# Sparse attention into a rational-activation MLP on one core: value matmuls grouped by row tile, casts let go batch by batch, first batch first, smaller groups and four banks at the ends

## The chip, the cores and the metric

The kernel runs on one core of one Trainium2 chip. The metric is the device time of one execution in microseconds (us). Profiles show the span of one execution, which is about 2 us shorter than the device time of the same run (595.4 against 597.3 us for the kernel before). All times in the text are medians unless they are read from one trace.

Engines: PE is TensorE, DVE is VectorE, ACT is ScalarE, POOL is GpSimd, SyncE (SP) issues DMA. "Granted clock" is the share of full speed that the profile shows for TensorE. A transfer "lands" when its semaphore reports it complete; it "starves" when it takes far longer to land than the same transfer does elsewhere in the trace, because others run beside it.

## The reference

Eight batches of 8 heads, 576 tokens, 64 columns. Heads 0 to 3 see a local band of 32 tokens, heads 4 to 7 every 32nd token. The result, 4608 x 512, goes through a two-layer MLP with a rational function in between.

```python
scores = (q @ k.T) / sqrt(D)                       # per batch and head
mask_local   = (rel >= 0) & (rel < 32)             # heads 0..3
mask_strided = (rel >= 0) & (pos_k % 32 == pos_q % 32)   # heads 4..7
attn = softmax(where(mask, scores, -1e9)) @ v      # B=8, H=8, S=576, D=64
x = attn.transpose(0, 2, 1, 3).reshape(4608, 512)
h = x @ w_in                                       # 512 -> 2048
P = a0 + a1*h + a2*h**2 + a3*h**3
Q = 1 + |b0|*|h| + |b1|*h**2
out = (P / (Q + 1e-6)) @ w_out                     # 2048 -> 512, fp32
```

## The kernel before

A list scheduler in the kernel file takes operations with an engine, dependences, an assumed cost and a priority key, and from them fixes the order of instructions on each engine. A change of a cost or of a dependence can therefore move many instructions.

For each of eight batches: POOL issues three casts (q, k, v from fp32 to bf16 copies in DRAM). SyncE loads from these copies: `ql` and `kl` re-layouts in DRAM (8 x 72 KB) and four transposes `qL`/`kL` from them for the local heads, four transposes `qS`/`kS` for the strided heads, 17 value loads. Then come scores on PE with Exp on ACT, five row tiles T = 0 to 4 of value matmuls into `psA`, a division on DVE into `XR`, and a DMA transpose of each tile into `XT`. Chunk c of the dense part is batch c's first 512 tokens; chunk 8 collects the 64 left-over tokens of all batches. "mm1" is `XT` times `Win` into `psH`; ACT evicts to `HB`; a chain of nine DVE operations (d1 to d9) with Ln and Exp on ACT makes the gate; "mm2" multiplies by `Wout` into `psO`.

```python
# the scheduler's model of a DMA: fixed latency after issue
end = free[e] + op.cost
op.end = end + op.lat

# all casts may start at once; so may the weights (POOL queue)
for b in range(B):
    for nm, s_, d_ in (("q", q, qc), ("k", k, kc), ("v", v, vc)):
        ...
        key = (b - 3) * P if b else -1000 + len(cast)
        add("POOL", <cast of the whole tensor of batch b>, [], 1.2, key, g, 5.0)
# Win: 4 loads, key -900; Wout: 4 loads, key 0.3 * P; neither waits for anything

def attend(b, evs):                     # matmul order inside one row tile T
    ...
    for h in range(4):                  # local heads
        makers.append(<128-row (T<4) or 64-row (T=4) matmul into psA[:, h]>)
        if T > 0:
            makers.append(<32-row matmul into the same psA[:, h]>)
    for h in range(4):                  # strided heads
        for g in range(4):
            if T < 4:
                makers.append(<128-row matmul into psA[32*g:32*g+32, 4+h]>)
            else:
                makers.append(<128-row matmul, 16 columns>)
                makers.append(<16-row matmul into the same place>)

# dense1: two groups of G = 8 column tiles per chunk; d9 writes a separate gate tile GB
# dense2: for each of four row blocks m: 16 matmuls into the one bank psO,
#         eviction on ACT, then 4 (last chunk: 8) stores issued by POOL
```

The softmax here doesn't subtract the row's maximum and nothing guards it: scores larger than these inputs give would overflow.

## Time and profile before

| | before |
|---|---|
| device time, median (lowest to highest) | 597.88 us (597.57 to 598.76), 3 runs |
| first score matmul | 113.5 us |
| first mm1 matmul / first DVE chain starts | 178.6 / 213.9 us |
| last chain ends / last store has landed / span ends | 567.3 / 591.3 / 595.4 us |
| DVE busy, PE busy over the span | 303.3, 390.4 us |

The page's second part cuts the span into 40 slices of 14.9 us; each digit is the busy share in tenths. Kernel before:

```profile
PE   0000000233349259899999999999999999998572
DVE  1000000000011049988869668768868986999910
PEclk9999999999999559999979979979979979999987
DMA  8999997546665542334625535532211211111202
```

For about seven slices DMA is nearly full and PE has nothing to do; DVE's first chain comes in slice 15. From slice 16 to near the end PE is full.

SyncE's timeline of the kernel before (start, duration in us, operation) shows what the full DMA did to the first loads:

```profile
7.51 40.92 SPq L461 DMA_DIRECT2D ql<-qc  x4
48.48 11.91 SPq L472 DMA_TRANSPOSE qS<-qc  x2
...
133.79 2.65 SPq L461 DMA_DIRECT2D ql<-qc  x4
```

The same four 72 KB loads occupy SyncE for 40.9 us while all casts are in flight, and 2.65 us later.

Windows of the kernel before (stretch, its length, then busy us of each engine with the number of instructions, granted clock, DMA share, GB/s):

```profile
core 0: us, PE busy (x) PEld busy (x) DVE busy (x) ACT busy (x) POOL busy (x), PEclk, DMA share, GB/s
0.00:114.00 114.00, 0.48 (x2) 0.13 (x2) 2.18 (x17) 1.28 (x1) 17.29 (x36) 1.00 0.96 187
380.00:425.00 45.00, 43.98 (x338) 21.75 (x343) 34.33 (x30) 31.15 (x35) 10.14 (x18) 0.92 0.30 55
515.00:567.00 52.00, 39.48 (x174) 16.40 (x175) 51.79 (x32) 39.33 (x39) 20.94 (x32) 0.97 0.17 41
```

In the middle stretch one batch takes 45 us and PE is busy for 44 of them, so PE sets the pace there; DMA is at 0.30. In the last one DVE is.

The same 45 us, counting only instructions that touch `psA` (the value matmuls of one batch):

```profile
core 0: us, PE busy (x) PEld busy (x) DVE busy (x), PEclk, DMA share, GB/s
380.00:425.00 45.00, 10.13 (x132) 6.63 (x132) 4.81 (x11) 0.92 0.30 55
```

PE's timeline of the kernel before around such a block: one block of 16 matmuls of the same shape, then the fifth row tile, where 128-row and 16-row matmuls alternate, and the matmuls behind it:

```profile
426.55 0.30 PE L520 MATMUL psA<-vs,ES 128*32 128x65 bf16 x16
...
433.17 0.20 PE L520 MATMUL psA<-vs,ES 128*16 128x65 bf16 x1
433.30 0.19 PE L520 MATMUL psA<-w,ES 16*16 16x65 bf16 x1
...
437.06 0.22 PE L520 MATMUL psA<-vs,ES 128*16 128x65 bf16 x1
437.21 0.22 PE L520 MATMUL psA<-w,ES 16*16 16x65 bf16 x1
437.77 1.49 PE L520 MATMUL psH<-XT,Win 128*128 128x512 bf16 x3 [0.34 <-issue]
439.05 1.91 PE L520 MATMUL psO<-Wout,GB 128*128 128x512 bf16 x4
```

Sixteen matmuls of one shape take 0.30 us; alternating ones start 0.13 to 0.15 us apart, so the 40 of the fifth tile take 5.3 us. It is not the second write into the same place of `psA` that costs: the step from a 16-row matmul to the next 128-row one, which writes another place, takes as long (0.12 to 0.15 us). Behind them a group of four 512-column matmuls takes 1.91 us where the usual is 1.03: the granted clock is 0.50 from 434.7 to 441.5 us, although PE was busy for 8.54 of the 8.70 us before that, at 1.00.

The tail of the kernel before, POOL's timeline:

```profile
574.71 15.25 POOL L799 DMA_DIRECT2D out_dram<-OS  x32 [11.80 <-issue]
```

The last 32 stores are issued one after the other, 7.4 us after the last chain's end (567.3).

### The profile page before, as it was taken

Reading aid. Unit: us, or ns where it says so; the run is one execution under the profiler, and the core shown is the slowest. Engines: PE = TensorE matmul, PEld = TensorE weight load, DVE = VectorE, ACT = ScalarE, POOL = GpSimd, SP = SyncE. Lnnn points to the kernel's source line nnn. Section 1 sums busy time; section 2 is a strip of 40 time slices with the busy share of each in tenths; the row PEclk is TensorE's granted clock in tenths of the full one; section 3 lists DMA queues with packets and bytes.
Section 4 is the critical chain, followed back from the end, with each engine's and each line's share of the span. In section 5 each row is a group of like instructions: output and inputs, shape, how many; then the busy total and the mean of one; then the engine's idle time right before and its main releaser. Section 6 shows DMA issues by size and latency. Waiting matters only on the chain.

```text
span 595.4 us, 6854 instructions
## 1 busy us (share of the span) xinstructions
PE 390.4 (66%) x2801; PEld 185.2 (31%) x2848; DVE 303.3 (51%) x259; ACT 272.3 (46%) x301; POOL 114.6 (19%) x196
## 2 busy tenths in 40 slices
PE   0000000233349259899999999999999999998572
PEld 0000000011124134454544544444454444443220
DVE  1000000000011049988869668768868986999910
ACT  0000000120104009976756757757756757988510
POOL 9200000000000000022213112212213222434336
PEclk9999999999999559999979979979979979999987
DMA  8999997546665542334625535532211211111202
GB/s 175 212 217 215 210 221 120 98 77 103 110 106 83 102 79 39 84 51 91 122 49 96 97 62 89 92 61 46 59 31 36 45 35 36 36 36 35 54 22 49
DMA packets 151839, 53.34 MB, mean 90 GB/s; under 512 B 145408, under 2 KB 147968, under 8 KB 151040
## 3 DMA queue, kind: packets, MB, share of 16 engines
q1 hardware_dynamic: 142848, 25.10, 25.3%
q0 software_dynamic: 8960, 27.80, 21.9%
q8 instruction: 22, 0.36, 0.3%
q14 instruction: 9, 0.07, 0.0%
HBM read 47.10 MB, written 28.31 MB: 127 GB/s over the span
## 4 chain that ended last, share of the span: by engine, by line
PE 46%; SPq 30%; DVE 10%; issue 4%; ACT 4%; POOL 3%; DMA 2%; DVEq 0%; POOLq 0%
PE psH L520 16%; PE psO L520 15%; PE psA L520 10%; SPq L461 9%; SPq L465 8%; SPq L472 5%; PE psS L520 4%; SPq L478 3%; POOL out_dram L799 3%; DVE GB L756 2%; DVE T L751 2%; DVE T L747 2%; ACT UU L737 1%; SPq L495 1%; DMA qc<-in_q_dram 1%
## 5 line engine op out<-in xcount | busy, mean ns | idle before, releaser
L791 POOL DMA_DIRECT2D out_dram<-OS x128 | 82.1, 647 | 462.5 <-ACT OS L784 462.1
L520 PE MATMUL psO<-Wout,GB 128*128 128x512 bf16 x551 | 147.3, 396 | 18.1 <-ACT OS L784 9.3
L520 PE MATMUL psH<-XT,Win 128*128 128x512 bf16 x558 | 146.9, 399 | 12.6 <-DMA XT<-XR 6.5
L716 ACT ACTIVATE HB<-psH 128x512 bf16<-128x512 f32 x144 | 82.5, 600 | 63.7 <-PE psH L520 62.6
L520 PE MATMUL psS<-MS,IDN 128*128 128x432 bf16 (+1 forms) x48 | 14.3, 386 | 130.7 <-DMA kL<-kl 128.8
L650 DVE RECIPROCAL RC<-psA 128x8 f32<-128x8 f32 x40 | 8.2, 205 | 180.0 <-PE psA L520 180.0
L567 ACT ACTIVATE ES<-psS 128x864 bf16<-128x864 f32 (+1 forms) x24 | 20.4, 849 | 143.9 <-PE psS L520 143.7
L520 PEld LDWEIGHTS psO<-Wout,GB 128*128 128x128 bf16 x576 | 54.8, 101 | 88.0 <-ACT OS L784 16.0
L520 PEld LDWEIGHTS psH<-XT,Win 128*128 128x128 bf16 x576 | 56.0, 102 | 81.0 <-issue 11.8
L737 ACT ACTIVATE UU<-UU,cst 128x2048 bf16<-128x2048 bf16 x36 | 71.7, 2001 | 4.2 <-DVE UU L730 4.2
L740 ACT ACTIVATE UU<-UU 128x2048 bf16<-128x2048 bf16 x36 | 68.8, 1911 | 0.1
L520 PEld LDWEIGHTS psS<-MS,IDN 128*128 128x128 bf16 x48 | 3.7, 101 | 134.4 <-DMA kL<-kl 128.9
L756 DVE TENSOR_TENSOR GB<-T,UU 128x4096 bf16<-128x4096 bf16 x18 | 41.1, 2284 | 4.1 <-ACT UU L740 3.9
L652 DVE TENSOR_TENSOR XR<-psA,RC 128x512 bf16<-128x512 f32 x40 | 27.4, 686 | 30.5 <-DMA XT<-XR 30.2
L751 DVE TENSOR_TENSOR T<-T,HB 128x4096 bf16<-128x4096 bf16 x18 | 41.1, 2283 | 0.3
L747 DVE TENSOR_TENSOR T<-T,HB 128x4096 bf16<-128x4096 bf16 x18 | 40.9, 2273 | 0.1
L730 DVE TENSOR_TENSOR UU<-UU,ZZ 128x4096 bf16<-128x4096 bf16 x18 | 40.9, 2271 | 0.0
L784 ACT ACTIVATE OS<-psO 128x512 f32<-128x512 f32 x36 | 21.4, 595 | 42.3 <-PE psO L520 42.2
L520 PE MATMUL psA<-vs,ES 128*32 128x65 bf16 (+1 forms) x640 | 37.1, 203 | 0.0
L724 DVE TENSOR_SCALAR ZZ<-HB 128x4096 uint16<-128x4096 uint16 x18 | 22.0, 1221 | 16.9 <-ACT HB L716 16.9
L520 PE MATMUL psA<-w,ES 16*16 16x65 bf16 x128 | 26.4, 206 | 0.0
L744 DVE TENSOR_SCALAR T<-HB,coef 128x4096 bf16<-128x4096 bf16 x18 | 24.1, 1339 | 0.0
(53 smaller groups left out, 295.2 us busy)
## 6 DMA issues: line engine op xcount, KB each, us to landing
out_dram<-OS POOLq DMA_DIRECT2D x128, 64.0 KB, 2.0
qc<-in_q_dram POOLq DMA_DIRECT2D x8, 576.0 KB, 43.6
kc<-in_k_dram POOLq DMA_DIRECT2D x8, 576.0 KB, 45.9
vc<-in_v_dram POOLq DMA_DIRECT2D x8, 576.0 KB, 48.2
ql<-qc SPq DMA_DIRECT2D x32, 72.0 KB, 2.8
kl<-kc SPq DMA_DIRECT2D x32, 72.0 KB, 2.8
Win<-in_moe_w_in_dram POOLq DMA_DIRECT2D x4, 512.0 KB, 17.0
Wout<-in_moe_w_out_dram POOLq DMA_DIRECT2D x4, 512.0 KB, 46.0
```

The source lines that it names most:

```text
L461: fn = (lambda e, b=b, pair=pair, hh=hh: e.dma_start(ql[b, pair].rearrange("(g p) c -> p g c", g=4)[:, :, 64 * hh:64 * hh + 64], qc[b, 2 * ...
L465: fn = (lambda e, b=b, pair=pair, hh=hh: e.dma_start(kl[b, pair, :, 64 * hh:64 * hh + 64], kc[b, 2 * pair + hh]))
L472: add("SP", (lambda e, src=src, dst=dst, b=b, sl=sl, gh=gh: e.dma_start_transpose(dst[sl][:, gh, :, :].rearrange("x h p -> x (h p)"), src[ ...
L520: return lambda e: e.matmul(out_ap, l, r, start=start, stop=stop, skip_group_check=True)
L716: o2 = add("ACT", (lambda a, hb=hb, hi=hi, fi=fi: a.activation(hb[:, fi, :], psH[hi][:, :], AF.Copy)), [o1, hb_free[ig % NHB]], 0.6, key - 30)
L730: d3 = add("DVE", (lambda d, u=u: d.tensor_tensor(u[:, :, :], u[:, :, :], ZZ[:, :, :], op=Alu.mult)), [d2], ctt, key + 0.02)
L737: ln = add("ACT", (lambda a, u=u, sl=sl: a.activation(u[:, sl, :], u[:, sl, :], AF.Ln, bias=cst[:, 0:1], scale=1.0)), [d3, cons], 0.28 + H ...
L740: ex = add("ACT", (lambda a, u=u, sl=sl: a.activation(u[:, sl, :], u[:, sl, :], AF.Exp, scale=-1.0)), [ln], 0.28 + HG * CH * 0.000833, key ...
L747: d5 = add("DVE", (lambda d, hb=hb, t3=t3: d.tensor_tensor(t3[:, :, :], t3[:, :, :], hb[:, :, :], op=Alu.mult)), [d4], ctt, key + 0.04)
L751: d7 = add("DVE", (lambda d, hb=hb, t3=t3: d.tensor_tensor(t3[:, :, :], t3[:, :, :], hb[:, :, :], op=Alu.mult)), [d6], ctt, key + 0.06)
L756: d9 = add("DVE", (lambda d, t3=t3, u=u, gb=gb: d.tensor_tensor(gb[:, :, :], t3[:, :, :], u[:, :, :], op=Alu.mult)), [d8, lns, g_free[ig % ...
L791: add("POOL", (lambda e, dst=dst, osl=osl, g=g: e.dma_start(dst[g], OS[osl][32 * g:32 * g + 32, :])), [ev], 0.3, base + m, go, 3.0)
```

## The change

The intent: start the first batch before the DMA is flooded, hold later casts back until the batch before has landed, and take PE's alternating matmuls away. Shorter groups at both ends are to let DVE start sooner and mm2 end sooner. The core of the diff (cuts marked with `...`; renamings, `NT3 = 6`, `NXT = 2`, and new assumed DMA costs are left out):

```diff
+            if op.group is not None:             # scheduler: DMAs share one ring
+                ring = max(ring, end) + op.lat
+                op.end = ring + 2.0
 ...
+    def casts(b):
+        dep = [tr_ev[b - 1], v_ev[b - 1]] if b else []     # all loads of batch b-1 have landed
+        key = (b - 3) * P if b else -1000.0
 ...                                             # batch 0: each tensor in two halves, strided heads first
+    def load_win():                              # Win in two halves; the second waits for tr_ev[0]
+    def load_wout():                             # waits for [tr_ev[1], v_ev[1]]
 ...
-        dep = [tr_ev[b]]                         # scores: the strided heads no longer wait
+        dep = [ts_ev[b]]                         # for the local heads' transposes
 ...
@@ attend(b, evs)
                 if T < 4:
-                    makers.append(mm(o, EL1[es][pair][:, hh, T, :], vt[iv][:, T, h, 0:65], True, T == 0))
+                    makers.append(mm(o, EL1[es][pair][:, hh, T, :], vt[iv][:, T, h, 0:65], h == 0, False))
 ...
+            for h in range(4):
+                pair, hh = divmod(h, 2)
                 if T > 0:
                     t = T - 1
-                    makers.append(mm(o, EL2[es][32 * t:32 * t + 32, hh, pair, 1, :, :].rearrange("x g c -> x (g c)"),
+                    makers.append(mm(psA[:, h, 0:65],
+                                     EL2[es][32 * t:32 * t + 32, hh, pair, 1, :, :].rearrange("x g c -> x (g c)"),
                                      vo[iv][32 * t:32 * t + 32, h, 0:65], False, True))
 ...
-                    if T < 4:
-                        makers.append(mm(psA[32 * g:32 * g + 32, 4 + h, 0:65],
-                                         ES[es][:, j, c0:c0 + 32], vs[iv][:, h, g, 0:65], True, True))
-                    else:
-                        o = psA[32 * g:32 * g + 16, 4 + h, 0:65]
-                        makers.append(mm(o, ES[es][:, j, c0:c0 + 16], vs[iv][:, h, g, 0:65], True, False))
+                    makers.append(mm(psA[32 * g:32 * g + M, 4 + h, 0:65],
+                                     ES[es][:, j, c0:c0 + M], vs[iv][:, h, g, 0:65], h == 0, False))
+            if T == 4:
+                for h in range(4):
+                    for g in range(4):
                         l0 = 8 * NP + 16 * h
-                        makers.append(mm(o, ES[es][32 * g:32 * g + 16, j, l0:l0 + 16],
+                        makers.append(mm(psA[32 * g:32 * g + 16, 4 + h, 0:65],
+                                         ES[es][32 * g:32 * g + 16, g % 2, l0:l0 + 16],
                                          w4[iv][32 * g:32 * g + 16, h, 0:65], False, True))
 ...
+    def sizes(c):
+        return [4, 4, 8] if c == 0 else [8, 4, 4] if c == NCH - 1 else [8, 8]
 ...
-            d9 = <gb = t3 * u>                   # separate gate tile
+            d9 = <t3 = t3 * u>                   # in place
 ...
+        tail = c == NCH - 1
+        if tail:                                 # last mm2: four banks instead of one
+            banks = [(psO[:, :], ...), (psA[:, 0:4, :]..., ...),
+                     (psA[:, 4:8, :]..., ...), (psS[:, 0, :], ...)]
 ...                                              # evictions alternate between ACT and DVE
```

## The prediction

> **What bounds the kernel now.** Three phases, read from the windows, the timeline and the chain of waits.
> (1) 0–114 us: DMA share 0.96 and no score matmul. All 24 casts and both weights are queued in the first 18 us. Behind them the first four 72 KB `ql` loads occupy SyncE for 40.9 us; later four take 2.65 us. The Trainium skill ("DMA: Bandwidth & Descriptors", Queues, rings and completion order) says that each DMA engine alternates between its queues packet by packet, and this starvation agrees.
> (2) 114–213 us: SyncE issues loads of later batches ahead of the `XT` transposes; the first mm1 runs at 178.6 and the first DVE chain at 213.9.
> (3) To 567 us the dense part. From 290 to 470 a batch takes about 45 us with PE busy 44, DVE 32–37, ACT 31: PE-bound. From 490 to 567 DVE is back to back (about 15 us per 8-tile chain). Then 28 us of last mm2 and 32 stores at 0.48 us.
>
> **What the change does.**
> - Value matmuls. In the timeline the fifth row tile alternates 128-row and 16-row matmuls at 0.126–0.15 us, 5.3 us for 40; 16 `vs` matmuls of one mode take 0.30 us. The skill ("TensorEngine Tiling (Array Packing)", Key Properties) says that changing the mode drains the array; the trace agrees. Grouped, I estimate 1.2 us for the fifth tile and 0.85 instead of 1.3 for tiles 2–4: about 5.5 us per batch. After the 5 us block the granted clock halves, and about 11 matmuls take 0.43 us instead of 0.216; a short block should save most of that, 2 us more. PE per batch: 45 → about 37. DVE keeps 35.6, ACT 33.6: three engines near 90%.
> - Casts by batch. First batch's casts take about 11 us at the traced 200 GB/s, then half of Win; its loads, at traced issue times (transpose 1.3, `ql`/`kl` 0.65, 17 value loads 9.2 us), end near 45 instead of 112. But the emitted order puts the last first-batch `XT` transposes behind the second batch's loads, which wait for its casts, issued only when batch 0 has landed. I estimate the first mm1 at 85 us (178 before) and the first chain at 90.
> - The new cost: each batch now repeats cast (about 10 us, in which SyncE's transfers starve) → loads (10.4 + 9.2 + 5.2 us) + `XT` (6.5 us) + landing. About 38–42 us in series. I expect this, not PE, to set the pace in the first half, worst for batch 2, where Wout adds 10 us; DVE idles in places until about 140 us.
> - Tail. Four banks remove about 5 us of 28; stores stay serial (15 us plus 5 us). Smaller groups add under 3 us of DVE.
>
> **Sum.** mm1 of batch 1 at about 136; then about 39 us per batch, seven steps, to about 409; last batch's chains about 34, tail 22: **465 us**, range 440–492 (8 in 10). Faster by over 2%: 0.98; within: 0.01; slower: 0.01.
>
> **What would show it.** First score matmul near 15–20 us, first mm1 at 75–95. Value matmuls' PE busy well under half. `XT` waits on PE and long SyncE gaps at casts, once per batch; granted clock above 0.93. DVE idle before ZZ (waiting ACT/PE) up, mostly before 200 us.
>
> **What would make it wrong.** If transfers hardly starve beside a single batch's casts, the cycle is nearer 32 us and DVE (303 us busy) sets the time: about 435. If POOL's in-order stores hold up casts, or PE stalls cool the clock repeatedly, 490 or more.

## The result, and the profile after

The changed kernel takes 509.89 us (508.04 to 511.21, 4 runs) against 598.06 us of the kernel before (597.57 to 598.76, 4 runs). Its ratio is 0.852 (95% interval 0.849 to 0.855). A ratio here is the mean time of one kernel's runs over the mean of the other's runs of the same rounds, so it is not quite the ratio of the medians. Executions over 1.5% slower than the fastest of the same kernel are left out of the means. The change is clearly faster, but by 88 us and not by the 133 that were predicted; 509.89 lies outside 440 to 492.

The same slices of the changed kernel (12.7 us each):

```profile
PE   0124334853389828979997699699999998898800
DVE  1000200869308671888595579749999999999700
PEclk9999999975579957997997899899999999999965
DMA  8947954897479669759848858955112310111030
```

PE starts 90 us sooner (first score matmul at 23.1 instead of 113.5 us) and DVE's first chain 124 us sooner (89.4 instead of 213.9). But where the kernel before had a full PE line and a DMA line of 2 to 5, PE, DVE and the clock now have notches up to slice 28, and DMA stays at 4 to 9. From slice 29 DMA is nearly idle, and PE and DVE are full up to the tail. Slice 29 starts at 355 us, and the last batch's loads have landed at 351.6.

The chain that ended last, by line, in the kernel before and in the changed kernel:

```profile
PE psH L520 16%; PE psO L520 15%; PE psA L520 10%; SPq L461 9%; SPq L465 8%; SPq L472 5%; PE psS L520 4%; SPq L478 3%; POOL out_dram L799 3%; DVE GB L756 2%; DVE T L751 2%; DVE T L747 2%; ACT UU L737 1%; SPq L495 1%; DMA qc<-in_q_dram 1%
```

```profile
PE psH L543 15%; DMA XT<-XR 15%; PE psO L543 10%; PE psS L543 4%; SPq L494 4%; POOL out_dram L807 3%; SPq L500 3%; PE psA L543 3%; DVE T L785 3%; DVE T L780 3%; DVE T L776 2%; DMA qc<-in_q_dram 2%; SPq L482 2%; DMA kL<-kl 2%; SPq L510 2%
```

Most of the `ql` and `kl` loads (L461 and L465 before, 9% and 8%; of their successors only L482 is listed, with 2%) and most of the value matmuls (`psA`, 10% to 3%) have left the chain. A new item stands in second place: in 15% of the span the chain goes through the landing of an `XT<-XR`, a transpose that moves 128 KB.

Windows of the changed kernel, two steps of the loads and two stretches behind the last load:

```profile
core 0: us, PE busy (x) PEld busy (x) DVE busy (x) ACT busy (x) POOL busy (x), PEclk, DMA share, GB/s
185.00:229.00 44.00, 35.62 (x320) 15.86 (x320) 27.98 (x25) 26.30 (x30) 8.41 (x15) 0.85 0.80 133
270.00:311.00 41.00, 35.24 (x316) 15.48 (x314) 27.75 (x24) 24.22 (x27) 13.82 (x19) 0.89 0.79 143
352.00:395.00 43.00, 41.88 (x379) 19.95 (x377) 40.35 (x35) 33.49 (x39) 11.40 (x20) 1.00 0.24 52
395.00:440.00 45.00, 40.40 (x220) 17.64 (x219) 43.35 (x28) 40.12 (x41) 15.41 (x25) 1.00 0.18 42
```

No engine is full in the first two: PE 81 and 86%, DVE 64 and 68%. With DMA out of the way PE is at 97 and 90%, DVE at 94 and 96%.

The value matmuls of one batch in the changed kernel, and its fifth row tile:

```profile
229.00:270.00 41.00, 3.73 (x132) 2.94 (x132) 3.77 (x9) 0.00 (x0) 0.92 0.73 134
```

```profile
218.00 0.30 PE L543 MATMUL psA<-vs,ES 128*16 128x65 bf16 x16
218.23 0.29 PE L543 MATMUL psA<-w,ES 16*16 16x65 bf16 x16
218.46 0.82 PE L543 MATMUL psO<-Wout,T 128*128 128x512 bf16 x3
```

10.13 us of PE have become 3.73, and three 512-column matmuls behind the block take 0.82 us, at full clock.

Now one step of the loads. POOL's casts of two batches, then SyncE between them, then the chain at that place:

```profile
229.27 1.28 POOL L450 DMA_DIRECT2D qc<-in_q_dram  x1 [6.90 <-DMA kL<-kl]
269.77 0.50 POOL L450 DMA_DIRECT2D qc<-in_q_dram  x1 [15.60 <-DMA kL<-kl]
```

```profile
227.47 2.57 SPq L694 DMA_TRANSPOSE XT<-XR  x2
235.67 3.34 SPq L494 DMA_TRANSPOSE qS<-qc  x2
...
261.44 1.32 SPq L694 DMA_TRANSPOSE XT<-XR  x1
...
266.73 1.27 SPq L500 DMA_TRANSPOSE kL<-kl  x1
268.04 4.91 SPq L694 DMA_TRANSPOSE XT<-XR  x3
276.08 2.28 SPq L494 DMA_TRANSPOSE qS<-qc  x1
```

```profile
268.04 2.52 DMA XT<-XR
270.66 13.43 DMA XT<-XR
284.13 1.04 PE psH L543 x4
...
312.19 14.04 DMA XT<-XR
326.28 3.41 PE psH L543 x8
```

The reader should see a loop. A batch's casts go when the previous batch's last `kL` has landed (269.5). SyncE waits about 6.5 us for the q copy, issues for some 32 us, and the last `kL` lands, which lets the next casts go. The last three `XT` transposes of the chunk stand directly behind that `kL` on SyncE, so the next casts (3 x 576 KB) are released just as they are issued. The third, which landed in 2.5 us elsewhere, takes 13.4 and 14.0 us here, in chunks 4 and 5, and mm1 of the chunk waits for it. It is not so in every step: the same transpose of chunks 2, 3 and 6 took 7.4, 2.5 and 2.4 us.

The tail of the changed kernel, POOL's timeline:

```profile
480.67 13.92 POOL L807 DMA_DIRECT2D out_dram<-OS  x29 [9.76 <-ACT OS L847]
```

The first store follows the last chain (478.6) after 2.0 us instead of 7.4. The last store has landed at 497.8, yet the span ends at 507.6: POOL's closing drain instruction takes 9.4 us; in the kernel before it took 3.7.

Comparing the sum of the prediction with what the trace shows, term by term (the starts of mm1 are read at its first eviction to `HB`; the measured sum is the span, 2 us under the device time):

| term | predicted | measured | miss |
|---|---|---|---|
| until mm1 of batch 1 | 136 | 139.9 | +4 |
| seven steps to mm1 of chunk 8 | 273 (39 each) | 435.7 - 139.9 = 295.8 (42.3 each) | +23 |
| last chains | 34 | 478.6 - 435.7 = 42.9 | +9 |
| tail | 22 | 507.6 - 478.6 = 29.0 | +7 |
| sum | 465 | 507.6 | +43 |

### The profile page after: what moved, and what is told of

It reads as the page before. It is cut to its first block, busy times and chain, and to the rows that moved or that the text cites. A ratio compares the mean times of both kernels' runs of the same rounds, so it can differ in the third digit from the quotient of the medians.

```text
span 507.6 us, 6925 instructions
## 1 busy us (share of the span) xinstructions
PE 350.3 (69%) x2848; PEld 155.5 (31%) x2848; DVE 306.5 (60%) x279; ACT 272.3 (54%) x299; POOL 118.1 (23%) x197
## 3 DMA queue, kind: packets, MB, share of 16 engines
q1 hardware_dynamic: 142848, 25.10, 31.7%
q0 software_dynamic: 9488, 27.80, 26.9%
## 4 chain that ended last, share of the span: by engine, by line
PE 32%; SPq 20%; DMA 19%; DVE 17%; issue 4%; ACT 3%; POOL 3%; DVEq 0%; POOLq 0%
PE psH L543 15%; DMA XT<-XR 15%; PE psO L543 10%; PE psS L543 4%; SPq L494 4%; POOL out_dram L807 3%; SPq L500 3%; PE psA L543 3%; DVE T L785 3%; DVE T L780 3%; DVE T L776 2%; DMA qc<-in_q_dram 2%; SPq L482 2%; DMA kL<-kl 2%; SPq L510 2%
## 5 line engine op out<-in xcount | busy, mean ns | idle before, releaser
L543 PE MATMUL psH<-XT,Win 128*128 128x512 bf16 x576 | 152.1, 403 | 29.8 <-DMA XT<-XR 27.8
L543 PE MATMUL psO<-Wout,T 128*128 128x512 bf16 x528 | 136.9, 391 | 15.2 <-ACT OS L847 6.7
L543 PEld LDWEIGHTS psO<-Wout,T 128*128 128x128 bf16 x528 | 48.7, 100 | 78.0 <-ACT OS L847 11.3
L785 DVE TENSOR_TENSOR T<-T,UU 128x4096 bf16<-128x4096 bf16 (+1 forms) x20 | 41.3, 2067 | 17.2 <-ACT UU L769 17.0
L753 DVE TENSOR_SCALAR ZZ<-HB 128x4096 uint16<-128x4096 uint16 (+1 forms) x20 | 22.3, 1114 | 47.9 <-ACT HB L745 47.9
L780 DVE TENSOR_TENSOR T<-T,HB 128x4096 bf16<-128x4096 bf16 (+1 forms) x20 | 41.4, 2070 | 0.2
L776 DVE TENSOR_TENSOR T<-T,HB 128x4096 bf16<-128x4096 bf16 (+1 forms) x20 | 41.3, 2067 | 0.1
L759 DVE TENSOR_TENSOR UU<-UU,ZZ 128x4096 bf16<-128x4096 bf16 (+1 forms) x20 | 41.2, 2058 | 0.0
L543 PE MATMUL psS<-ML,IDN 128*128 128x512 bf16 (+1 forms) x48 | 15.9, 419 | 35.2 <-DMA kL<-kl 33.0
L756 DVE TENSOR_SCALAR UU<-ZZ,coef 128x4096 bf16<-128x4096 bf16 (+1 forms) x20 | 24.6, 1232 | 0.0
L773 DVE TENSOR_SCALAR T<-HB,coef 128x4096 bf16<-128x4096 bf16 (+1 forms) x20 | 24.6, 1231 | 0.0
```

The source lines that it names most:

```text
L543: return lambda e: e.matmul(out_ap, l, r, start=start, stop=stop, skip_group_check=True)
L756: d2 = add("DVE", (lambda d, gn=gn, u=u: d.tensor_scalar(u[:, 0:gn, :], ZZ[:, 0:gn, :], b1_ap, b0_ap, op0=Alu.mult, op1=Alu.add)), [d1, ev ...
L759: d3 = add("DVE", (lambda d, gn=gn, u=u: d.tensor_tensor(u[:, 0:gn, :], u[:, 0:gn, :], ZZ[:, 0:gn, :], op=Alu.mult)), [d2], ctt, key + 0.02)
L773: d4 = add("DVE", (lambda d, gn=gn, hb=hb, t3=t3: d.tensor_scalar(t3[:, 0:gn, :], hb[:, 0:gn, :], a_ap[3], a_ap[2], op0=Alu.mult, op1=Alu. ...
L776: d5 = add("DVE", (lambda d, gn=gn, hb=hb, t3=t3: d.tensor_tensor(t3[:, 0:gn, :], t3[:, 0:gn, :], hb[:, 0:gn, :], op=Alu.mult)), [d4], ctt ...
L780: d7 = add("DVE", (lambda d, gn=gn, hb=hb, t3=t3: d.tensor_tensor(t3[:, 0:gn, :], t3[:, 0:gn, :], hb[:, 0:gn, :], op=Alu.mult)), [d6], ctt ...
```

## The experiments

The question was why the steps take 42 us and not 39, and more widely what holds PE below its pace of 36 to 37. The quoted expectations use short names for the theories. From here on d1 and d2 are the names of two runs, not the DVE operations of the chain. S: the cycle is slow because its parts stand in series, each batch's casts waiting for the last landing. F: the transfers themselves, casts beside SyncE's many small ones, are what takes the time, so that their total matters and not how early a cast is let go. O: the static orders of PE and DVE set the pace and transfers do not. C: the casts alone cost, SyncE's loads do not. D: the whole loop of casts, loads and `XT` sets the pace of mm1. In the runs called "orders same" the instruction orders of the other engines are those of the changed kernel.

Each edit is against the changed kernel unless it says otherwise. All results are correct except for the two that are wrong. One run each of e1, e3 and e9 was slow; the ratios leave it out, the medians in the table do not. The medians of their fast runs are 529.93, 525.71 and 509.24 us. The kernel before took 597.8 to 599.2 us.

| run | median us (lowest to highest) | ratio to before (95%) |
|---|---|---|
| changed kernel | 509.89 (508.04 to 511.21) | 0.852 (0.849 to 0.855) |
| e1_two_ahead | 531.32 (525.43 to 542.64) | 0.884 (0.878 to 0.891) |
| e2_no_throttle | 554.38 (553.00 to 555.53) | 0.926 (0.923 to 0.929) |
| e3_values_old | 526.47 (523.79 to 531.81) | 0.878 (0.874 to 0.882) |
| e4_before_grouped | 545.19 (544.88 to 546.58) | 0.911 (0.909 to 0.914) |
| e5_small_runs | 507.84 (504.63 to 508.98) | 0.847 (0.843 to 0.851) |
| d1_no_vloads (wrong) | 465.56 (461.41 to 468.26) | 0.780 (0.776 to 0.783) |
| d2_no_casts (wrong) | 470.68 (469.94 to 473.28) | 0.787 (0.784 to 0.790) |
| e8_tail_stores | 502.55 (500.77 to 504.37) | 0.839 (0.836 to 0.841) |
| e9_plain_ends | 509.81 (508.12 to 517.56) | 0.850 (0.848 to 0.852) |
| v_direct | 455.73 (454.62 to 456.20) | 0.761 (0.759 to 0.764) |
| v_direct_tail | 450.01 (448.60 to 451.39) | 0.751 (0.749 to 0.753) |
| v_best | 446.21 (443.84 to 448.49) | 0.746 (0.744 to 0.748) |

### e1_two_ahead: let casts go one batch sooner

```diff
-        dep = [tr_ev[b - 1], v_ev[b - 1]] if b else []
+        dep = [tr_ev[max(b - 2, 0)], v_ev[max(b - 2, 0)]] if b else []
```

> Casts of batch b wait for the landing of batch b-2 instead of b-1; the orders of all engines are scheduled anew. Theory S (serial chain: the landing of one batch releases the next batch's casts, and the loads wait for these): landings of the last kL, 40 to 44 us apart from batch 2 on in the changed kernel, come 33 to 37 us apart; total 475 to 490 us. Rival F (flood: the loads starve while casts run, whoever waits for whom): the casts of a later batch now run beside the loads, landings stay 40 us apart or more, total 500 to 515.

Measured: 531.32 us, 20 us slower in the fast runs (529.93). From batch 1 to batch 7 the last `kL` landed at 120.1, 136.0, 201.6, 222.1, 261.4, 304.9 and 339.5 us: first in pairs, then, from batch 4 to 7, 39.1 us apart, where the changed kernel has 40.9. The last landing is 12 us sooner than in the changed kernel (351.6). But batch 1 landed at 120 instead of 90 (the casts of batches 1 and 2 and the second half of Win were all released when batch 0 landed, at 43 us), and mm1 of batch 1 came at 184.8 instead of 139.9. That start lost 45 us; the seven steps to mm1 of chunk 8 regained 17 of them (278.9 against 295.8), and the end 5 (67.3 us to the end of the span instead of 72.0).

What follows: a throttle one batch looser does not free the pipeline. S, which expected a gain, falls as it was put. F had the pace nearly right and the total wrong (it missed by at least 15 us), because it left the start out. As this edit moves both the start and the steps, it could not settle the cause.

### e5_small_runs: the same casts in shorter contiguous runs

```diff
-  d_[b]....rearrange("(r c) -> r c", c=2048)              # and the same for s_[b]
+  d_[b]....rearrange("(x y c) -> y x c", y=16, c=512)     # batches 1 to 7, orders same
```

> The casts of batches 1 to 7 move the same bytes in runs of 512 elements instead of long contiguous ones; same waits, same orders of all engines. Rival F with starvation by packet size: SyncE's transfers get a larger share beside the casts, the XT transposes of chunks 4 and 5, which took 13 to 14 us to land, land in under 6, landings of batches come 35 to 38 us apart, total 480 to 495. If packet size does not matter: XT landings as before, total 505 to 515. If small runs slow the casts themselves (landing of v over 15 us after issue instead of 12): total over 515.

Measured: 507.84 us, 2 us less, with intervals that overlap. In the two chunks above the last `XT` took 11.4 and 8.1 us from issue to landing instead of 13.4 and 14.0. The edit cut each of these 21 casts into 576 packets of 1 KB where the changed kernel has 32 of 18 KB (POOL's queue: 20912 packets for the same 27.80 MB, instead of 9488). The first of the two transposes in this kernel's chain, and the chain by line:

```profile
268.77 11.38 DMA XT<-XR
```

```profile
PE psH L543 12%; PE psO L543 9%; DMA XT<-XR 8%; SPq L500 5%; SPq L494 4%; PE psS L543 4%; SPq L518 3%; DVE T L785 3%; SPq L510 3%; POOL out_dram L807 3%; DVE T L780 3%; DMA kL<-kl 3%; DVE T L776 3%; SPq L526 3%; SPq L482 2%
```

What follows: packets an eighteenth as long relieve the transposes only in part (13.4 to 11.4, 14.0 to 8.1 us). What makes the rest stays open. And a share of the chain is not a gain: `XT` fell in it from 15% to 8%, 34 us less, and the time by 2 us, because SyncE's loads took its place in the chain and the landings stayed 41.5 us apart.

### e3_values_old and e4_before_grouped: the value matmuls by themselves

```diff
 # e3: the changed kernel with the matmul list of attend() of the kernel before
 # e4: the kernel before with the matmul list of attend() of the changed kernel
 # only the order inside each row tile on PE differs in either
```

> The changed kernel with the old order of the value matmuls; all engines but PE have the same order. If the DMA cycle sets the pace of the first half, PE has 5 us or so of slack in each 41 us, and the 8 us of PE time that come back per batch cost only 1 to 3 us each: total 515 to 530. Rival (PE sets the pace, so the grouping is worth its whole PE time): total 555 or more.

> The kernel before with only the value matmuls grouped; same orders. The PE-bound stretch from 290 to 470 us goes from 45 to 38-40 us per batch, the start does not move (first mm1 near 179 us), and VectorE, which needs about 303 us from its first chain at 214 us, becomes the limit: total 560 to 575. The granted clock no longer halves after the fifth row tile. If the grouping gives nothing because another engine limits: 590 or more.

Measured: taking the grouping out of the changed kernel costs 15.8 us (525.71, the fast runs of e3, against 509.89), as expected. Putting the grouping into the kernel before gains 53.8 us (598.95 to 545.19). That is 15 us more than the most that was expected: the steps fell to 36 us, not to 38 to 40. Windows of e4 in its steady stretch:

```profile
336.00:372.00 36.00, 35.15 (x336) 17.18 (x341) 33.81 (x29) 30.30 (x35) 10.18 (x16) 1.00 0.62 102
372.00:408.00 36.00, 35.15 (x336) 17.18 (x341) 33.81 (x29) 30.31 (x36) 10.17 (x16) 1.00 0.24 52
```

A batch takes 36 us instead of 45, PE is busy for 35.15 of them, and the granted clock is 1.00 instead of 0.92, with nothing else changed. The prediction's "PE per batch: 45 → about 37" is confirmed by this run, a little on the good side, and so is the claim that the granted clock falls with the alternating block. In the changed kernel the same grouping is worth less than a third of that; PE does not set the pace there until the last loads have landed, as d1 and d2 show below. The gains of the parts do not add up: 54 for the grouping alone, 73 for everything else alone (598.95 to 525.71), 88 for both.

### d2_no_casts: the casts' traffic taken away from batch 2 on (wrong result)

```diff
+        # b >= 2: the cast moves only rows 0..15, columns 0..63 of the [r, 2048] view
+        # loads of batch b read qc/kc/vc[b % 2]; same instructions, same waits, orders same
```

> Wrong result on purpose: from batch 2 on a cast moves only 16 rows of 64 elements, and the loads read the copies of batch 0 or 1; orders and waits as in the changed kernel. Theory D (the DMA cycle of cast, loads and XT sets the pace of mm1 until the last batch has landed): landings of batches come 31 to 34 us apart instead of 41, XT transposes land in under 4 us instead of 13, mm1 of batches 1 to 6 starts 36 to 38 us apart instead of 45, which is the pace of the grouped kernel without throttled casts; total 455 to 475. Rival O (the fixed orders of PE and SyncE hold mm1, not the DMA time): pace stays over 42, total over 495.

Measured: 470.68 us, 39 us less than the changed kernel (relative error 0.044, from reading old batches). The landings of the last `kL` came 35.1 us apart from batch 2 on and mm1 38.5 us apart, each slightly above what was expected. The last `XT` of the same two chunks landed in 4.0 and 3.4 us. Its chain by line:

```profile
PE psH L549 20%; PE psO L549 16%; PE psS L549 7%; PE psA L549 4%; DVE T L791 3%; POOL out_dram L813 3%; SPq L506 3%; DMA XT<-XR 3%; DVE T L786 3%; SPq L500 3%; DMA kL<-kl 2%; DVE UU L765 2%; DVE T L782 2%; ACT UU L772 2%; SPq L488 2%
```

`DMA XT<-XR` has gone from 15% to 3% and PE stands first again. In this trace the chain from 210 to 245 us passes through almost nothing but PE.

### d1_no_vloads: 16 of the 17 value loads taken away from batch 2 on (wrong result)

```diff
+        if b >= 2:
+            dropped.extend(gv.ops[1:])      # removed after scheduling; the rest of the orders same
```

> Wrong result on purpose: from batch 2 on only one of the 17 value loads is issued; casts, waits and all other orders as in the changed kernel. Theory D: SyncE is free of about 8.5 us per batch, landings come 32 to 35 us apart, the XT transposes still starve beside the casts (10 us or more to land for chunks 4 and 5), total 465 to 485. Rival C (only the casts' time matters, the loads hide): landings stay 40 us apart, total over 500.

Measured: 465.56 us, 44 us less (relative error 0.043). The landings came 31.3 us apart. The last `XT` still took 10.5 and 9.9 us. But PE no longer waits for much: from 200 to 300 us it is busy for 96.9 of 100, at a granted clock of 1.00.

What follows from d1 and d2 together: with the orders of PE, DVE and ACT untouched, shortening the loop of cast, loads and landing, by 6 us (41.4 to 35.1) on the side of the casts or by 10 (to 31.3) on the side of the loads, brings the time to that of the prediction. O falls: the orders allow 466. C falls: the casts are not alone, as the loads' share is worth as much. The loop as a whole sets the pace in the changed kernel. The starving of the last `XT` does not do it by itself: d1 left most of it in place and gained more than d2, which removed it. The two gains of about 40 us would probably not add up either (no run tried both): in d1 the landings are 31.3 us apart and mm1 is at 36.0, PE's own pace.

### e2_no_throttle: casts not held back at all

```diff
-        dep = [tr_ev[b - 1], v_ev[b - 1]] if b else []
+        dep = []
```

> The changed kernel without the throttle: casts wait for nothing, first batch still split and first; orders scheduled anew. The first batch's loads starve until about 90 us, first mm1 between 120 and 180 us, then 36 to 37 us per batch; total 500 to 550. If the throttle costs more than it gives: under 500.

Measured: 554.38 us, 4 us above what was expected. First mm1 eviction at 195.5 us (expected between 120 and 180), later even than in the kernel before (180.5). The throttle is thus worth 44 us in this kernel, at a price: it makes the loop that d1 and d2 measured. Without it everything else in the change is 9 us slower than the grouping alone in the kernel before (545.19).

### v_direct: no copy of v, values loaded straight from the input

```diff
-        for nm, s_, d_ in (("q", q, qc), ("k", k, kc), ("v", v, vc)):
+        for nm, s_, d_ in (("q", q, qc), ("k", k, kc)):
 ...
-            add("SP",   <17 value loads from vc[b]>, ...)
+            add("POOL", <17 value loads from v[b], cast in the DMA>, ...)   # rescheduled
```

> A try at a better version: the value tiles are loaded and cast by GpSimd straight from v, so the copy of v and 17 SyncE loads per batch go away; orders scheduled anew. If Theory D holds and these loads of short runs take under 15 us per batch: landings of kL 31 to 35 us apart, total 455 to 480. If short cast runs are slow (over 20 us per batch) or GpSimd's order blocks: over 500.

Measured: 455.73 us. This takes from the loop what d1 and d2 took away, in part and without a wrong result: a third of the casts' bytes and all 17 issues from SyncE. The last `kL` landings are 31.7 us apart from batch 2 on, and mm1 of the first chunk comes at 74.4 us instead of 84.7. It is no saving of DMA time: POOL's queue takes 47.1% of the 16 DMA engines' span instead of 26.9. mm1 now lags the landings, with 39.1 us from chunk to chunk (chunks 1 to 6).

### e8_tail_stores and e9_plain_ends: the tail

```diff
 # e8: of the last chunk's 32 stores, the 16 with bb = 1 are issued by SyncE (orders else same)
-                    add("POOL", <store>, ..., go, 0.1)
+                    add("SP" if bb else "POOL", <store>, ..., gsp if bb else go, 0.1)
```

```diff
 # e9: neither the smaller groups nor the four banks (rescheduled)
-        return [4, 4, 8] if c == 0 else [8, 4, 4] if c == NCH - 1 else [8, 8]
+        return [8, 8]
-        tail = c == NCH - 1
+        tail = False
```

> The changed kernel with 16 of the 32 stores of the last chunk issued by SyncE instead of GpSimd; all orders else the same. If the serial issue on GpSimd (0.48 us each) is what the tail consists of, the end comes 7 to 8 us earlier: total 500 to 504, and the last chain ends where it did (near 479 us). If GpSimd's closing drain (9.4 us in the changed kernel, 3.7 in the one before) is what counts and does not shrink or hide: gain the same 7 to 8 us, the drain still 9 us; if the drain grows when it starts earlier: gain under 3 us.

> The changed kernel with chain groups of eight everywhere and the last mm2 in one bank as before: what the two end parts of the change are worth. Orders scheduled anew. First chain 3 to 4 us later, but the DMA cycle sets the pace after it, so nothing of that remains; the last chain ends within 4 us of the changed kernel's, and the last mm2 takes 17 us instead of 4, of which 12 of the stores' 15 us hide behind it: total 512 to 520. If the parts are worth nothing: 508 to 512.

Measured: e8 gains 7.3 us (502.55): the last store lands at 488.5 instead of 497.8, and the drain still takes 9.6 us. e9 is as fast as the changed kernel, 509.81 against 509.89, so the two parts of the change at the ends bring nothing together. Its trace shows why. With a single bank the four row blocks come 4.3 us apart, and a block's eight stores take about 3.9 us, so the stores take 16.9 us from the first to the last instead of 15.8 with four banks: little is left to save. And the last chain ends at 474.3 without small groups, 478.6 with them. From there to the end of the last issue it is 21.8 us without the four banks and 17.8 with them, so the banks save 4.0 us behind the chain and the groups lose 4.3 before it. Why the groups lose can be argued from the code: a third group in the last chunk reuses the `HB` buffer of the first (there are two), and its last eviction comes at 465.9 instead of 449.9. That was not tested by itself.

### v_direct_tail and v_best: the parts that helped, together

```diff
 # v_direct_tail = v_direct + e8's edit
 # v_best        = v_direct_tail + e5's edit for the casts of q and k
```

> The better version with the last chunk's stores split between GpSimd and SyncE: 7 to 8 us less than it, 447 to 450; all else as there. If the closing drain eats it: 453 or more.

> As v_direct_tail, with the casts of q and k in runs of 512 elements. The first test of small runs changed the total by about 2 us, so 444 to 450; slower than 452 if the small runs hold up the value loads on GpSimd's queue.

Measured: 450.01 and 446.21 us, both as expected (450.01 at the edge of 447 to 450). v_best is 12% below the changed kernel and 25% below the kernel before. Its slices (11.0 us each):

```profile
PE   0031527954799979999999939999999997998930
DVE  1000210999069967988997991889999999999910
DMA  8997999999997997998996999222132101112130
```

DMA is nearly full up to slice 25, where the loads end (the last `kL` landed at 274.1; 351.6 in the changed kernel), and from slice 12 on PE is full beside it in all but two slices. The chain agrees: PE has 51% of it (32% in the changed kernel), SyncE's issues and the DMA together 16% (39%). So the landings no longer set the pace; PE's own work mostly does.

## Why the prediction was right or wrong

**The step that failed** is, in the prediction's words, "then about 39 us per batch, seven steps, to about 409". The mechanism it rests on was named correctly ("this, not PE, to set the pace"). The term was mis-sized, and it lasted longer than "in the first half". Measured: 42.3 us on average, in two parts. From chunk 1 to 6 mm1 came 44.8 us apart, (363.8 - 139.9) / 5; the last two steps took 35.9 each, after the last load had landed at 351.6. The five are uneven: 54.5, 39.8, 51.0, 42.8 and 35.8 us.

The miss of 23 us can be taken apart with the landings. Five landings from batch 2 to 7 took 41.4 us each, (351.6 - 144.8) / 5, against 39: 12 us. In the same five steps mm1 slipped from 5 us ahead of the next batch's landing (139.9 and 144.8) to 12 us behind it (363.8 and 351.6): 17 us. The last two steps gave 6 back. The prediction's own sum of the cycle was "38–42 us in series", and the landings kept to it; what the sum left out is that mm1 does not keep step with them. It also had not seen that the chunk's last `XT` transposes are issued just as the landing releases the next casts: it counted 6.5 us for the five, and in chunks 4 and 5 the last one alone took 13 to 14. That this starving makes the slip is not shown, and d2 speaks against it as the whole cause: there the last `XT` landed in 4.0 and 3.4 us, and mm1 slipped by 17 us all the same (from 133.3 against a landing at 138.2 to 325.6 against 313.5), with PE's own work in the chain. What makes the slip in the changed kernel stays open; the clock, 0.90 over these five steps and 0.96 in d2, is another candidate that no run tested by itself. What d1 and d2 do show is broader: that the loop as a whole, with casts and loads, holds the time at 510 instead of about 466 to 471.

**The last chains** were put at 34 us and took 43. DVE is busy for 42.7 of these 42.9 us. The last chain of chunk 7 ends only at 448.6, 13 us after chunk 8's first eviction, and chunk 8's own three chains take the other 30: DVE was working off a queue that the prediction had not counted. **The tail** was put at 22 and took 29. The four banks do save about what was estimated ("about 5 us of 28": from the last chain to the end of the last issue 22.6 us in the kernel before, 17.8 in the changed one), but a closing drain longer by 5.7 us takes it back, and e9 shows that the ends as a whole are worth nothing. The longer drain does not come from the ends: it is 9.5 us in e9, which lacks them, and 3.7 in e2, which has them but no throttle.

**Right:** first mm1 at 85 (82.8 measured), first chain at 90 (89.4), first batch's loads at 45 (41.8), mm1 of batch 1 at 136 (139.9). The grouping: 5.5 us per batch estimated, 6.4 measured (10.13 to 3.73), and the clock with it (e4: 0.92 to 1.00). Two sentences of the Trainium skill carried this. "TensorEngine Tiling (Array Packing)", Key Properties, says that a change of mode drains the array; the traces agree (0.13 to 0.15 us per alternating matmul, 16 of one shape in 0.30). "DMA: Bandwidth & Descriptors", Queues, rings and completion order, says that each DMA engine takes turns between its queues packet by packet; the starving agrees with it (40.9 against 2.65 us, 13.4 against 2.5), but e5, with packets an eighteenth as long, relieved it only in part. On the same page, Issuing engines are not separate DMA queues says that transfers from all engines share the same 16 DMA engines and interleave; here SyncE's queue takes 31.7% and POOL's 26.9% of the same 16 engines' span (page of the changed kernel).

**Wrong in small:** the first score matmul ran at 23.1 us, not at 15 to 20. The granted clock was not above 0.93 but 0.906 on average: 0.85 and 0.89 in the two windows of the loads, in which PE is idle for 19 and 14% of the time, and 1.00 behind the last load. The prediction had named this as a way to "490 or more"; how much of the miss it makes was not tested. Its other way did not happen: from batch 3 on POOL issued each q cast within 0.3 us of the landing of the last `kL` that it waited for. DVE's idle time did not end mostly before 200 us; it lasted until the loads had ended. And "nearer 32 us [...] about 435" would have been too hopeful: with the landings at 31.3 us apart, d1 took 466, with mm1 at 36.0 us from chunk to chunk and PE busy for 96.9 of 100 us: PE is the next limit.

## What to carry to other kernels

Before adding a throttle, write down the loop that it closes (release, transfer, issue, landing, release), and look at which instructions stand right behind the one whose landing releases the next flood: here they starved, though e5 and d2 do not show that this by itself cost the time. A gain on an engine is worth its full size only while this engine sets the pace; here the same grouping was worth 54 us in one kernel and 16 in the other. When a loop of transfers sets the pace, removing a transfer altogether (v_direct, 54 us) beat every re-timing of it that was tried.

## What the Trainium skill lacked or had wrong

- "TensorEngine Tiling (Array Packing)" says that a change of mode drains the array, with no cost. Here alternating 128-row and 16-row matmuls of 65 columns start 0.13 to 0.15 us apart, against about 0.015 us each in a block of 16 of one shape (218.00 to 218.23 us).
- "TensorE: Matmul & The Clock Gate" ties the clock to how busy the array is and does not say how a run of such small alternating matmuls counts. Here the 5.3 us block was followed by matmuls at half speed (four in 1.91 instead of 1.03 us), though PE had been busy for 8.54 of the 8.70 us before the clock fell, and grouping alone took the clock of the steady stretch from 0.92 to 1.00 (e4).
- "DMA: Bandwidth & Descriptors" gives the turn-taking between queues but no size for what a small transfer loses beside a bulk cast. Here a transpose of 128 KB took 13.4 and 14.0 us instead of 2.5 beside 3 x 576 KB of casts, and packets of 1 KB instead of 18 KB brought this only to 11.4 and 8.1.
- No page that was read tells the length of POOL's closing drain after its last store: 3.7 us in the kernel before, 9.4 in the changed one, 9.6 with half the last stores moved to SyncE, 2.0 in e1 and 3.7 in e2. In the runs whose casts wait for the batch just before, it was 9.2 to 9.7. What sets it stays open.
